# Grouped attention with all output stored in 256 B rows, and the last K block loaded in two halves

## The chip, the cores and the metric

The kernel runs on one core of a Trainium2 chip. The metric is the device time in microseconds (us) of one execution. One core has a matrix engine (PE), a vector engine (DVE), a scalar engine (ACT), a general engine (POOL) and SyncE (SP), which here only issues DMAs; 16 DMA engines move the data.

## The reference, cut to what matters

```python
B, Hq, Hkv, Sq, Sk, D = 16, 32, 8, 16, 2048, 128      # q, k, v in bf16
k = jnp.repeat(k, 4, axis=1);  v = jnp.repeat(v, 4, axis=1)
scores = jnp.einsum("bhqd,bhkd->bhqk", q, k) * D ** -0.5
return jnp.einsum("bhqk,bhkd->bhqd", softmax(scores, axis=-1), v)
```

There are 16 x 8 = 128 pairs of batch and key head. Each pair has 64 query rows, 2048 keys and 2048 values. K and V are 64 MiB each, q and the output 2 MiB each, so the work is mostly a stream of K and V through the chip.

## The kernel before, in words

**Tiling.** The pairs are taken four at a time: 32 quads, numbered n. A quad's K is one DMA of 2 MiB into one of three buffers (`Kn`, `load_k`), its V two DMAs of 1 MiB into one of four buffers (`Vb`, `load_v`). Each quad makes two steps, so there are 64 steps; step 2n works on the first half of the keys, step 2n+1 on the second half.

**A step on the engines.** DVE transposes a half of K (`kt`, L450, two instructions). PE multiplies it with the query matrix (`S`, L372 and L317). DVE scales and negates the scores out of PSUM and finds their minimum (`negated`, L463). ACT takes exponentials (L579). PE transposes the probabilities (`PT`, L392), ACT evicts them (L591), and PE multiplies them with V (`PV`, L421). Five steps lie between the scores of a step and its PV. When a quad's two PVs are done, ACT (in the last steps DVE, `norm`, L535) multiplies the sums by the reciprocal row sums and writes an output buffer `Osb` (L602).

**The query.** For every four quads, POOL lays q out with masks (`lay_q`, L178), PE folds and transposes it (`Q`, L350), and ACT evicts it (`qe`, L567 and L570).

**The output.** There are NO = 8 output buffers. A quad's output is 256 rows of 256 B. For quads below PAIRED = 28 the query rows are arranged so that two neighbouring output rows come out in partitions 32 apart; POOL copies one beside the other (`join`, L198, two copies per quad), and the two stores of the quad (`store_part`, L191) then move 64 pieces of 512 B each. Quads 28 to 31 are stored without joining, in 128 pieces of 256 B per store.

**The order on SP.** SP issues all loads and nearly all stores, in one order written out by a loop over t = 0 to 63 + SLAG (L288). At even t it issues the K of quad t/2, when the buffer's transposes are done; at t = p + 6, or p + 7 from p = 24 on, half p of V, when the PV of the quad four before is done; at even t from SLAG = 20 on, the two stores of quad (t - 20)/2, when its joins are done. The whole last V comes at t = 70 in three pieces of 16, 12 and 4 key blocks (`LASTV`, L265). So the stores of quads 0 to 24 stand ahead of the last V, and those of 25 to 31 behind it. The last store's second half goes out from ACT's own queue.

Of the kernel before, what the change touches and what calls it, by code (L numbers as in the profile page):

```python
# [6 lines left out]
ACT = mybir.ActivationFunctionType  # L7
ALU = mybir.AluOpType
# [4 lines left out]
NK = 3  # L13
# [1 line left out]
NKT = 2  # L15
NS = 3
NPT = 4
NO = 8
NQ = 2
VLAG = (6, 7)  # L20
VFAR = 24
PVLAG = 5
SLAG = 20
PAIRED = 28
QLOAD = (0, 1, 5)
QLEAD = 13
TURNS = 8
# [3 lines left out]
NMBASE = 8  # L31
# [6 lines left out]
def bass_standalone__gqa_softmax__sampling_kernel(  # L38
# [29 lines left out]
    Sneg = [sb(f"Sneg{i}", [128, Sk], F32) for i in range(NS)]  # L68
    P = [sb(f"P{i}", [128, 16, 2, 64], F32) for i in range(2)]
    PT = [sb(f"PT{i}", [128, 8, 128], F32) for i in range(NPT)]  # L70
    Osb = [sb(f"O{i}", [128, 2, 2, 128], BF16) for i in range(NO)]
    nhalf = sb("nhalf", [128, 2, RING], F32)
    nbias = sb("nbias", [128, RING], F32)
    rowsum = sb("rowsum", [128, RING], F32)
# [4 lines left out]
    def col(x, p):  # L79
        return x[:, p % RING:p % RING + 1]  # L80
# [33 lines left out]
    sem_e2 = sem("sem_e2")  # L114
    sem_nm = sem("sem_nm")
    sem_nl = sem("sem_nl")
    sem_pc = sem("sem_pc")

    qf = q.rearrange("b h s d -> (b h s) d")
    of = out.rearrange("b h s d -> (b h s) d")  # L120
# [49 lines left out]
    def pt_ap(h, i):  # L170
        return PT[h % NPT][:, 4 * i:4 * (i + 1), :].rearrange("p t q -> p (t q)")

    def lay_q(eng, c, rs=range(4)):
        if rs[0] == 0:
            eng.wait_ge(sem_q[c % NQ], 16 * (c // NQ + 1))
        src = Qn[c % NQ][:, :, :].rearrange("p j (b x) -> p (j b) x", b=2)
        for r in rs:
            eng.tensor_scalar(  # L178
                Q4[:, :, :, r, :].rearrange("p j b x -> p (j b) x"), src,
                mask[:, r:r + 1], None, op0=ALU.mult,  # L180
            ).then_inc(sem_q4, 1)

    def store_part(eng, n, c):
        rows = of[256 * n + 128 * c:256 * n + 128 * (c + 1), :]
        if n < PAIRED:
            dst = rows.rearrange("(x r l) d -> r x (l d)", x=2, l=2)
            src = Osb[n % NO][64 * c:64 * c + 32, :, :, :].rearrange("p x l d -> p x (l d)")
        else:
            dst = rows.rearrange("(x r) d -> r x d", x=2)
            src = Osb[n % NO][64 * c:64 * (c + 1), :, 0, :]  # L190
        eng.dma_start(dst, src).then_inc(sem_o[n % NO], 16)  # L191

    def join(eng, n):
        eng.wait_ge(sem_nm, NMBASE + 2 * n + 2)
        for c in range(2):
            if 2 * n + c >= 1:
                eng.wait_ge(sem_pc, 2 * n + c)
            eng.tensor_copy(  # L198
                Osb[n % NO][64 * c:64 * c + 32, :, 1, :], Osb[n % NO][64 * c + 32:64 * (c + 1), :, 0, :],
            ).then_inc(sem_pc, 1)  # L200

    with nc.Block() as block:

        @block.gpsimd
        def _(gp):
            gp.iota(iota_m[:, :, :], [[-8, 4], [-32, 4]], base=0, channel_multiplier=1).then_inc(sem_id, 1)
            gp.iota(iota_t[:, :], [[1, 128]], base=0, channel_multiplier=-1).then_inc(sem_id, 1)
            gp.wait_ge(sem_id, 2)
            gp.tensor_scalar(ident4[:, :], iota_t[:, :], 0.0, None, op0=ALU.is_equal).then_inc(sem_id, 1)
            gp.tensor_scalar(lo_m[:, :, :], iota_m[:, :, :], 0.0, None, op0=ALU.is_ge).then_inc(sem_id, 1)  # L210
            gp.tensor_scalar(hi_m[:, :, :], iota_m[:, :, :], 8.0, None, op0=ALU.is_lt).then_inc(sem_id, 1)
            gp.wait_ge(sem_id, 5)
            gp.tensor_tensor(lo_m[:, :, :], lo_m[:, :, :], hi_m[:, :, :], op=ALU.mult).then_inc(sem_id, 1)
            for x in range(2):
                gp.wait_ge(sem_id, 6 + x)
                a = lo_m[:, :, :] if x == 0 else hi_m[:, :, :]
                w = 2 >> x
                dst = hi_m[:, :, 0:2] if x == 0 else mask[:, :].unsqueeze(2)
                gp.tensor_tensor(dst, a[:, :, 0:w], a[:, :, w:2 * w], op=ALU.add).then_inc(sem_id, 1)
            gp.wait_ge(sem_id, 8)  # L220
            id4 = ident4[:, :].rearrange("p (u i r) -> p u i r", u=4, i=4)
            gp.tensor_tensor(half_m, id4[:, :, 0:2, :], id4[:, :, 2:4, :], op=ALU.add).then_inc(sem_id, 1)
            gp.wait_ge(sem_id, 9)
            gp.tensor_tensor(fold[:, :, :], half_m[:, :, 0, :], half_m[:, :, 1, :], op=ALU.add).then_inc(sem_id, 1)
            gp.sem_inc(sem_nm, NMBASE)
            for c in range(1, NQC):
                gp.wait_ge(sem_stq, 2 * c)
                if c >= 3:
                    gp.wait_ge(sem_pc, 8 * c - 16)
                lay_q(gp, c, (0, 1))  # L230
                if c >= 2:
                    gp.wait_ge(sem_q4, 4 * c + 2)
                    join(gp, 4 * c - 8)
                    gp.wait_ge(sem_pc, 8 * c - 14)
                lay_q(gp, c, (2, 3))
                if c >= 2:
                    gp.wait_ge(sem_q4, 4 * c + 4)
                    for n in range(4 * c - 7, 4 * c - 4):
                        join(gp, n)
            for n in range(4 * NQC - 8, PAIRED):  # L240
                join(gp, n)

        @block.sync
        def _(sp):
            def load_k(n):
                s = n % NK
                if n >= NK:
                    sp.wait_ge(sem_kt, 2 * (n - NK) + 2)
                sp.dma_start(Kn[s][:, :], kf[n]).then_inc(sem_k[s], 16)

            def load_v(p):
                n, c = divmod(p, 2)
# [20 lines left out]

            def store(n):
                s = n % NO
                if n < PAIRED:
                    sp.wait_ge(sem_pc, 2 * n + 2)
                elif n < NQD - 2:
                    sp.wait_ge(sem_nm, NMBASE + 2 * n + 2)
                elif n == NQD - 2:  # L280
                    sp.wait_ge(sem_nl, 3)
                else:
                    sp.wait_ge(sem_nm, NMBASE + 2 * (NQD - 2) + 1)
                    sp.wait_ge(sem_nl, 4)
                for c in range(2 if n < NQD - 1 else 1):
                    store_part(sp, n, c)

            for t in range(NT + SLAG):  # L288
                if t == 4:
                    sp.sem_inc(sem_exp, EXPBASE)  # L290
                    sp.sem_inc(sem_e2, TURNS - 1)
                for c in range(NQC):
                    if t == (QLOAD[c] if c < len(QLOAD) else 8 * c - QLEAD):
                        load_q(c)
                if t < NT and t % 2 == 0:
                    load_k(t // 2)
                for p in range(NT):
                    if t == p + VLAG[p >= VFAR]:
                        load_v(p)
                if t >= SLAG and t % 2 == 0:  # L300
                    store((t - SLAG) // 2)
            for s in range(NO):
# [3 lines left out]
        def _(pe):  # L306
# [18 lines left out]
            def emit(op, turn=False):  # L325
# [11 lines left out]
                elif op[0] == "Q":  # L337
# [6 lines left out]
                        wait(sem_ev[b], 8 * c - 4, 8, turn)  # L344
                    dst = ST_ps[:, 512 * b:512 * (b + 1)]
                    src = Q4[:, :, :, :, :].rearrange("p j b i (x e) -> p j b e (i x)", e=2)
                    dst = dst.rearrange("p (u l r j e) -> p j l e u r", u=4, l=2, r=8, j=4)
                    for j in range(8):
                        for e in range(2):
                            ins = pe.matmul(  # L350
                                dst[:, j // 2, j % 2, e], src[:, j, b, e, :], fold[:, :, :], start=True, stop=True)
                    ins.then_inc(sem_stq, 1)
                elif op[0] == "S":
                    _, n = op
# [90 lines left out]
        def _(dve):  # L445
            def kt(n, e, k_at=None):
                Q, x = divmod(n, 2)
                if x == 0 and e == 0:
                    dve.wait_ge(sem_k[Q % NK], 16 * (Q // NK + 1) if k_at is None else k_at)
                ins = dve.transpose(  # L450
                    KT[n % NKT][:, :].rearrange("p (t b g e a) -> p e g t b a", t=8, b=2, g=2, e=2)[:, e],
                    Kn[Q % NK][:, :].bitcast(F32).rearrange(
# [77 lines left out]
            def norm(n, xs, done):  # L530
# [2 lines left out]
                dve.wait_ge(sem_pv, 2 * n + 2)  # L533
                for x in xs:
                    dve.tensor_scalar(  # L535
                        Osb[n % NO][:, x, 0, :], o_ap(n, x), col(rrec, 2 * n + x), None, op0=ALU.mult).then_inc(done, 1)

            def evict(h, halves):
                for i in halves:
# [19 lines left out]
        def _(act):  # L559
            for op in act_prog:  # L560
                if op[0] == "qe":
                    _, c, b = op
                    act.wait_ge(sem_stq, 2 * c + b + 1)
                    dst = QT[:, b, :, :, :].rearrange("p u q e -> p (u q e)")
                    src = ST_ps[:, 512 * b:512 * (b + 1)]
                    if 4 * c < PAIRED:
                        ins = act.activation(dst, src, ACT.Copy)  # L567
                    else:
                        for l in range(2):
                            ins = act.activation(  # L570
                                dst.rearrange("p (u r l e) -> p l u r e", u=4, l=2, e=2)[:, l],
                                src.rearrange("p (u l r e) -> p l u r e", u=4, l=2, e=2)[:, l], ACT.Copy)
                    ins.then_inc(sem_qe, 1)
                elif op[0] == "exp":
                    p, lo, hi = op[1], *(op[2:] or (0, 16))
                    n, x = divmod(p, 2)
# [18 lines left out]
                else:  # L595
                    _, n, x = op
                    if x == 0:
                        act.wait_ge(sem_rec, n + 1)
                        if n >= NO:
                            act.wait_ge(sem_o[n % NO], 32 * (n // NO))  # L600
                        act.wait_ge(sem_pv, 2 * n + 2)
                    act.activation(Osb[n % NO][:, x, 0, :], o_ap(n, x), ACT.Copy,  # L602
                                   scale=col(rrec, 2 * n + x)).then_inc(sem_nm, 1)
            act.wait_ge(sem_nm, NMBASE + 2 * (NQD - 2) + 1)
            act.wait_ge(sem_nl, 4)
# [29 lines left out]
```

## Time and profile before

| | |
|---|---|
| median of 3 runs | 337.86 us (337.86 to 337.90) |
| the profiled execution, its own time | 337.53 us |
| its span, first to last instruction | 335.7 us |
| busy: PE, DVE, ACT, POOL | 280.0, 308.0, 220.6, 104.1 us |
| DMA packets and bytes | 21151 packets, 138.62 MB, mean 413 GB/s |
| join copies, POOL L198 | 56, mean 393 ns |

All times inside the span count from its first instruction. The device time is 1.8 us longer than the span. A busy share is an average over the span; what sets the end is read from the chain of waits, which goes back from the last instruction, at each step to what released it. A packet is what one DMA engine moves at a time; the trace lists for each its queue, start, duration and size, and for each DMA when its semaphore was raised (it landed).

### The profile page before, as it was taken

The page shows a single profiled execution, that of the slowest core. Times are in us where ns is not written, and L with a number is a line of the kernel's source. Part 1 is how long each engine was busy: PE and PEld are TensorE (multiplying, and loading weights), DVE is VectorE, ACT ScalarE, POOL GpSimd, SP SyncE. Part 2 cuts the span into 40 slices and gives each one's busy share as a digit, 9 for nine tenths or more (in the row PEclk, how much of TensorE's full clock was granted, in tenths as well). Part 3 has the DMA queues.
Part 4 walks back from the last instruction along what each step waited for, and adds up shares of the span by engine and source line. Part 5 has one row for each costly group of instructions (what it writes and reads, how often), then busy time and mean ns, then how long its engine had stood idle before and what let it go on. Part 6 is the DMA issues. An engine that isn't in the chain of part 4 may idle for free.

```text
span 335.7 us, 14448 instructions
## 1 busy us (share of the span) xinstructions
PE 280.0 (83%) x6959; PEld 158.3 (47%) x5893; DVE 308.0 (92%) x465; ACT 220.6 (66%) x331; POOL 104.1 (31%) x98
## 2 busy tenths in 40 slices
PE   7877678888988899888988898878877979777895
PEld 2013344445545555455644554444543545444575
DVE  1999998998999999999999999899999999999872
ACT  2044666766787677766777677756767757567671
POOL 3840037300680029400680029400592000000000
PEclk9999999999999999999999999999999999999999
DMA  7999999999999999999999999999999999999995
GB/s 293 443 418 428 424 416 412 423 424 426 415 420 418 424 431 422 423 428 417 414 428 427 424 424 414 422 427 429 422 419 420 423 427 428 420 427 412 422 411 177
DMA packets 21151, 138.62 MB, mean 413 GB/s; under 512 B 3728, under 2 KB 7568, under 8 KB 9104
## 3 DMA queue, kind: packets, MB, share of 16 engines
q1 hardware_dynamic: 20992, 138.39, 99.3%
q8 instruction: 9, 0.15, 0.2%
q10 hardware_dynamic: 144, 0.03, 0.1%
q14 instruction: 6, 0.05, 0.0%
HBM read 136.31 MB, written 2.10 MB: 412 GB/s over the span
## 4 chain that ended last, share of the span: by engine, by line
DVE 49%; DMA 28%; PE 17%; issue 3%; ACT 2%; DVEq 0%
DMA Kn<-in_k_dram 27%; DVE Sneg L463 25%; DVE KT L450 22%; PE S_ps L372 5%; PE S_ps L317 4%; PE O_ps L421 3%; PE ST_ps L392 2%; PE ST_ps L350 2%; ACT P L579 1%; PE O_ps L317 1%; DMA Qn<-in_q_dram 1%; PE S_ps L421 1%; DVE Q L178 1%; ACT PT L591 0%; DVE nbias L472 0%
## 5 line engine op out<-in xcount | busy, mean ns | idle before, releaser
L450 DVE STREAM_TRANSPOSE KT<-Kn 128x1024 f32<-128x1024 f32 x128 | 151.0, 1218 | 10.3 <-DMA Kn<-in_k_dram 10.3
L463 DVE TENSOR_SCALAR_CACHE_REDUCE Sneg<-S_ps 128x1024 f32<-128x1024 f32 x128 | 149.9, 1205 | 4.9 <-PE S_ps L317 4.4
L579 ACT ACTIVATE P<-Sneg,nbias 128x2048 bf16<-128x2048 f32 (+1 forms) x66 | 129.0, 1955 | 15.4 <-DVE nbias L472 15.2
L372 PE MATMUL S_ps<-KT,QT 32*64 32x512 bf16 x1024 | 106.5, 387 | 35.4 <-DVE Sneg L463 34.4
L591 ACT ACTIVATE PT<-ST_ps 128x512 f32<-128x512 f32 x123 | 66.7, 597 | 60.2 <-PE ST_ps L392 60.2
L317 PE MATMUL S_ps<-KT,QT 32*64 32x512 bf16 x1024 | 106.0, 381 | 0.0
L178 POOL TENSOR_SCALAR Q<-Qn,mask 128x1024 bf16<-128x1024 bf16 x28 | 79.2, 2842 | 48.3 <-PE ST_ps L350 42.2
L372 PEld LDWEIGHTS S_ps<-KT,QT 32*64 32x64 bf16 x1024 | 34.8, 103 | 104.3 <-issue 91.3
L421 PEld LDWEIGHTS O_ps<-Vb,PT 64*64 64x64 bf16 x3968 | 58.0, 107 | 49.1 <-issue 48.7
L421 PE MATMUL O_ps<-Vb,PT 64*64 64x128 bf16 x3968 | 67.9, 218 | 14.4 <-DMA Vb<-in_v_dram 12.4
L198 POOL COPY O<-O 32x256 bf16<-32x256 bf16 x56 | 22.0, 393 | 163.9 <-ACT O L602 145.7
L392 PE MATMUL ST_ps<-ident,P 128*128 128x128 f32 x512 | 69.9, 280 | 0.2 <-ACT P L579 0.2
L392 PEld LDWEIGHTS ST_ps<-ident,P 128*128 128x128 f32 x512 | 54.8, 141 | 8.4 <-issue 2.6
L602 ACT ACTIVATE O<-O_ps,rrec 128x128 bf16<-128x128 f32 x56 | 17.5, 363 | 22.1 <-PE O_ps L421 22.1
L567 ACT ACTIVATE QT<-ST_ps 128x512 bf16<-128x512 f32 x14 | 7.7, 595 | 9.1 <-PE ST_ps L350 9.0
L579 ACT ACTIVATION_READ_ACCUMULATOR P<-Sneg,nbias 128x1 f32 x66 | 13.3, 201 | 0.0
L350 PEld LDWEIGHTS ST_ps<-fold,Q 128*128 128x128 bf16 x256 | 8.5, 101 | 7.9 <-issue 7.9
L317 PE MATMUL O_ps<-ident 128*128 128x512 bf16 x42 | 11.2, 415 | 0.0
L463 DVE DVE_READ_ACCUMULATOR Sneg<-S_ps 128x1 f32 x128 | 10.5, 82 | 0.0
L350 PE MATMUL ST_ps<-fold,Q 128*128 128x32 bf16 x256 | 9.4, 198 | 0.3 <-DVE Q L178 0.3
L472 DVE TENSOR_TENSOR nbias<-nhalf 128x2 f32<-128x2 f32 x32 | 5.3, 167 | 1.1
L459 DVE RECIPROCAL rrec<-rowsum 128x2 f32<-128x2 f32 x31 | 4.9, 159 | 0.0
(27 smaller groups left out, 19.9 us busy)
## 6 DMA issues: line engine op xcount, KB each, us to landing
Kn<-in_k_dram SPq DMA_DIRECT2D x32, 2048.0 KB, 18.2
Vb<-in_v_dram SPq DMA_DIRECT2D x63, 1024.0 KB, 21.4
Qn<-in_q_dram SPq DMA_DIRECT2D x8, 256.0 KB, 16.1
out_dram<-O SPq DMA_DIRECT2D x63, 32.0 KB, 19.8
Vb<-in_v_dram SPq DMA_DIRECT2D x1, 768.0 KB, 14.4
Vb<-in_v_dram SPq DMA_DIRECT2D x1, 256.0 KB, 14.6
out_dram<-O ACTq DMA_DIRECT2D x1, 32.0 KB, 2.0
```

What stands on the lines that cost most here:

```text
L178: eng.tensor_scalar(Q4[:, :, :, r, :].rearrange("p j b x -> p (j b) x"), src, mask[:, r:r + 1], None, op0=ALU.mult,).then_inc(sem_q4, 1)
L198: eng.tensor_copy(Osb[n % NO][64 * c:64 * c + 32, :, 1, :], Osb[n % NO][64 * c + 32:64 * (c + 1), :, 0, :],).then_inc(sem_pc, 1)
L317: return pe.add_instruction(mybir.InstMatmult(name=nc.get_next_instruction_name(), engine=mybir.EngineType.PE, ins=[pe.lower_ap(rhs), pe.l ...
L350: ins = pe.matmul(dst[:, j // 2, j % 2, e], src[:, j, b, e, :], fold[:, :, :], start=True, stop=True)
L372: ins = pe.matmul(s_ap, w, x, start=(acc == 0), stop=(acc == 3))
L392: ins = pe.transpose(dst[:, 128 * z:128 * (z + 1)], src[:, t, :], ident4[:, :])
L421: ins = pe.matmul(o_ap(n, x)[64 * c:64 * (c + 1), :], w[rows, c], Vb[n % NV][rows, c, key, :], start=(key == 0), stop=(key == 31),)
L450: ins = dve.transpose(KT[n % NKT][:, :].rearrange("p (t b g e a) -> p e g t b a", t=8, b=2, g=2, e=2)[:, e], Kn[Q % NK][:, :].bitcast(F32) ...
L463: ins = dve.tensor_scalar(Sneg[p % NS][:, 1024 * x:1024 * (x + 1)].rearrange("p (t a m) -> p t a m", t=8, m=4), S_ps[:, 1024 * y:1024 * (y ...
L579: ins = act.activation(P[n % 2][:, lo:hi, x, :].bitcast(BF16), Sneg[p % NS][:, 128 * lo:128 * hi].rearrange("p (t k) -> p t k", k=128), AC ...
L591: act.activation(pt_ap(h, i), stage_ap(h, i), ACT.Copy).then_inc(sem_ev[i], 1)
L602: act.activation(Osb[n % NO][:, x, 0, :], o_ap(n, x), ACT.Copy, scale=col(rrec, 2 * n + x)).then_inc(sem_nm, 1)
```

## The change

- The output is stored for all quads in rows of 256 B, 128 pieces per store. `join` goes from POOL, and the arrangement of the query rows that it needed goes from PE's `Q` and ACT's `qe`: PE now writes its folded query in runs of 32 columns, and ACT reorders while it evicts.
- There are ten output buffers in place of eight, and the stores come 24 steps behind the loads in place of 20. The stores of quads 0 to 22 then stand ahead of the last V and those of 23 to 31 behind it.
- The last K (quad 31) is loaded in two DMAs of 1 MiB, one for each step, each with two pieces of 4 KiB per partition. Between them goes the V half that followed the whole K before (half 55). The second half has its own semaphore.
- A start value of a semaphore is added by SP in place of POOL.

```diff
-NO = 8
+NO = 10
-SLAG = 20
-PAIRED = 28
+SLAG = 24
-    Osb = [sb(f"O{i}", [128, 2, 2, 128], BF16) for i in range(NO)]
+    Osb = [sb(f"O{i}", [128, 2, 128], BF16) for i in range(NO)]
     def store_part(eng, n, c):
-        rows = of[256 * n + 128 * c:256 * n + 128 * (c + 1), :]
-        if n < PAIRED:
-            dst = rows.rearrange("(x r l) d -> r x (l d)", x=2, l=2)
-            src = Osb[n % NO][64 * c:64 * c + 32, :, :, :].rearrange("p x l d -> p x (l d)")
-        else:
-            dst = rows.rearrange("(x r) d -> r x d", x=2)
-            src = Osb[n % NO][64 * c:64 * (c + 1), :, 0, :]
-        eng.dma_start(dst, src).then_inc(sem_o[n % NO], 16)
+        dst = of[256 * n + 128 * c:256 * n + 128 * (c + 1), :].rearrange("(x r) d -> r x d", x=2)
+        eng.dma_start(dst, Osb[n % NO][64 * c:64 * (c + 1), :, :]).then_inc(sem_o[n % NO], 16)
# SP, load_k and the loop over t
-                sp.dma_start(Kn[s][:, :], kf[n]).then_inc(sem_k[s], 16)
+                if n < NQD - 1:
+                    sp.dma_start(Kn[s][:, :], kf[n]).then_inc(sem_k[s], 16)
+                else:
+                    load_k_half(0)
+            def load_k_half(x):
+                n = NQD - 1
+                halves = lambda t: t.rearrange("a (g x y) -> a x g y", g=2, x=2)[:, x]
+                sp.dma_start(halves(Kn[n % NK][:, :]), halves(kf[n])).then_inc(sem_kl if x else sem_k[n % NK], 16)
                 for p in range(NT):
                     if t == p + VLAG[p >= VFAR]:
                         load_v(p)
+                if t == NT - 2:
+                    load_k_half(1)
# SP, store
-                if n < PAIRED:
-                    sp.wait_ge(sem_pc, 2 * n + 2)
-                elif n < NQD - 2:
+                if n < NQD - 2:
                     sp.wait_ge(sem_nm, NMBASE + 2 * n + 2)
# DVE, kt
+                if n == NT - 1 and e == 0:
+                    dve.wait_ge(sem_kl, 16)
```

More of the change, by code (lines that the diff above doesn't have):

```diff
@@ L116, in bass_standalone__gqa_softmax__sampling_kernel @@
     sem_nl = sem("sem_nl")
-    sem_pc = sem("sem_pc")
+    sem_kl = sem("sem_kl")
     qf = q.rearrange("b h s d -> (b h s) d")
@@ L171, in pt_ap, with lay_q @@
         return PT[h % NPT][:, 4 * i:4 * (i + 1), :].rearrange("p t q -> p (t q)")
-    def lay_q(eng, c, rs=range(4)):
-        if rs[0] == 0:
-            eng.wait_ge(sem_q[c % NQ], 16 * (c // NQ + 1))
+    def lay_q(eng, c):
+        eng.wait_ge(sem_q[c % NQ], 16 * (c // NQ + 1))
         src = Qn[c % NQ][:, :, :].rearrange("p j (b x) -> p (j b) x", b=2)
-        for r in rs:
+        for r in range(4):
             eng.tensor_scalar(
@@ L183, in store_part @@
     def store_part(eng, n, c):
-        rows = of[256 * n + 128 * c:256 * n + 128 * (c + 1), :]
-        if n < PAIRED:
-            dst = rows.rearrange("(x r l) d -> r x (l d)", x=2, l=2)
-            src = Osb[n % NO][64 * c:64 * c + 32, :, :, :].rearrange("p x l d -> p x (l d)")
-        else:
-            dst = rows.rearrange("(x r) d -> r x d", x=2)
-            src = Osb[n % NO][64 * c:64 * (c + 1), :, 0, :]
[L191 to L200, printed above, removed]
+        dst = of[256 * n + 128 * c:256 * n + 128 * (c + 1), :].rearrange("(x r) d -> r x d", x=2)
+        eng.dma_start(dst, Osb[n % NO][64 * c:64 * (c + 1), :, :]).then_inc(sem_o[n % NO], 16)
     with nc.Block() as block:
@@ L224, in _ @@
             gp.tensor_tensor(fold[:, :, :], half_m[:, :, 0, :], half_m[:, :, 1, :], op=ALU.add).then_inc(sem_id, 1)
-            gp.sem_inc(sem_nm, NMBASE)
             for c in range(1, NQC):
                 gp.wait_ge(sem_stq, 2 * c)
[L228 to L241, printed above, removed]
+                lay_q(gp, c)
         @block.sync
@@ L289, in _ @@
                 if t == 4:
+                    sp.sem_inc(sem_nm, NMBASE)
                     sp.sem_inc(sem_exp, EXPBASE)
@@ L346, in emit @@
                     src = Q4[:, :, :, :, :].rearrange("p j b i (x e) -> p j b e (i x)", e=2)
-                    dst = dst.rearrange("p (u l r j e) -> p j l e u r", u=4, l=2, r=8, j=4)
+                    mv = fold[:, :, :].rearrange("p u r -> p (u r)")
                     for j in range(8):
                         for e in range(2):
-                            ins = pe.matmul(
-                                dst[:, j // 2, j % 2, e], src[:, j, b, e, :], fold[:, :, :], start=True, stop=True)
+                            z = 2 * j + e
+                            ins = pe.matmul(dst[:, 32 * z:32 * (z + 1)], src[:, j, b, e, :], mv, start=True, stop=True)
                     ins.then_inc(sem_stq, 1)
@@ L535, in norm @@
                     dve.tensor_scalar(
-                        Osb[n % NO][:, x, 0, :], o_ap(n, x), col(rrec, 2 * n + x), None, op0=ALU.mult).then_inc(done, 1)
+                        Osb[n % NO][:, x, :], o_ap(n, x), col(rrec, 2 * n + x), None, op0=ALU.mult).then_inc(done, 1)
             def evict(h, halves):
@@ L563, in _ @@
                     act.wait_ge(sem_stq, 2 * c + b + 1)
[L564 to L573, printed above, removed]
+                    act.activation(
+                        QT[:, b, :, :, :].rearrange("p u (r j) e -> p (u r) (j e)", j=8),
+                        ST_ps[:, 512 * b:512 * (b + 1)].rearrange("p (z a) -> p a z", z=16), ACT.Copy,
+                    ).then_inc(sem_qe, 1)
                 elif op[0] == "exp":
@@ L601, in _ @@
                         act.wait_ge(sem_pv, 2 * n + 2)
-                    act.activation(Osb[n % NO][:, x, 0, :], o_ap(n, x), ACT.Copy,
+                    act.activation(Osb[n % NO][:, x, :], o_ap(n, x), ACT.Copy,
                                    scale=col(rrec, 2 * n + x)).then_inc(sem_nm, 1)
```

## The prediction

> **What bounds the kernel now.** First the page's slices and queues.
>
> ```profile
> DMA  7999999999999999999999999999999999999995
> ...
> q1 hardware_dynamic: 20992, 138.39, 99.3%
> ```
>
> From the second slice to the last but one the DMA engines are never idle, and SP's queue holds nearly all their time. What a DMA costs there moves everything behind it. Second, the chain of waits, its last 51 us (start, length, what).
>
> ```profile
> 284.80 23.30 DMA Kn<-in_k_dram
> 308.10 0.02 issue
> 308.12 2.37 DVE KT L450 x2
> 310.49 2.28 DVE Sneg L463 x4
> ...
> 312.87 2.36 DVE KT L450 x2
> 315.24 2.28 DVE Sneg L463 x4
> ...
> 328.07 2.06 PE O_ps L421 x128
> 330.13 0.32 issue
> 330.45 2.01 PE S_ps L421 x128
> ...
> 332.58 0.35 DVE O L535
> ```
>
> The last K lands at 308.10. DVE and PE work through it, the last PV (S_ps L421) ends at 332.46, the last output is scaled, and at 333.05 SP issues the last store, which lands at 335.26. The trace's landings show a second bound close by: the three pieces of the last V land at 328.82, 330.78 and 331.53, and PE needs them at 330.45, 331.45 and 332.2, only 0.7 us later for the latter two. Third, SP's own order of time and the group of stores (minimum/median/maximum ns).
>
> ```profile
> 300.07 4.94 SPq L191 DMA_DIRECT2D out_dram<-O  x2
> 305.90 1.64 SPq L258 DMA_DIRECT2D Vb<-in_v_dram  x2
> 307.58 3.18 SPq L191 DMA_DIRECT2D out_dram<-O  x2
> 315.96 1.90 SPq L265 DMA_DIRECT2D Vb<-in_v_dram  x3
> 317.91 15.73 SPq L191 DMA_DIRECT2D out_dram<-O  x13
> ```
> ```profile
> L191 SPq DMA_DIRECT2D out_dram<-O x63: 425/433/4315, 83.1 to 333.0; - x63
> ```
>
> A store's issue takes 0.43 us, but some last up to 4.3 us without waiting for a semaphore: the first behind the last V 3.18 us (317.91 to 321.10). I counted the packets that SP had issued and no engine had started: in such issues those of all earlier DMAs come to 70 to 83 per engine when the issue ends. I read that as a queue that takes no more. One thing more: the stores of 256 B at 327.62, 328.26, 330.92 and 333.05 take 0.59 to 0.63 us to issue, with little queued for the last two.
>
> **Part by part. The stores.** Packets of 512 B take 27.2 ns among the loads. The first 105 packets of 256 B, in the full queue at 329 us, take 18.0 ns each. The landings of K lie 9.88 us apart without stores and 10.06 with a quad's two. Packet durations give these times if each packet overlaps the next by 3.6 ns: 256 x 309.4 + 128 x 612.4 + 48 x 5.4 ns over 16 engines is 9.87 us, and a quad's stores 128 x 23.6 + 32 x 5.4 over 16 add 0.20. In rows of 256 B a quad costs 256 x 14.4 + 32 x 5.4 over 16 = 0.24 us. Bounds: 11.8 ns (half a 512 B packet) gives 0.20, as before; 23.6 ns (as long as a 512 B packet) gives 0.39; the mean of all 256 B packets of this queue, 20.9 less 3.6, gives 0.29. I take 14.4, the row in the full queue.
>
> Two quads of stores fewer stand ahead of the end's loads. Ahead of the last V: 23 x 0.24 - 25 x 0.20 = +0.55 us. The last K in pieces of 4 KiB: 512 x (160.5 - 3.6) against 128 x 612.4 ns, over 16, +0.12. So the last V is 0.7 us later. The K of quad 30 (stores of 18 quads ahead, not 20) is 0.35 later, the last K 0.4.
>
> **The last K.** Before, DVE is done with quad 30's steps at 307.52 and idles 0.60 us until 308.12. Quad 30's work now ends at 307.9. The first half, 256 x 156.9 ns over 16 = 2.5 us after the V that ends at 303.2 + 0.4, lands at 306.1, so DVE goes straight on at 307.9, 0.25 earlier than before. The second half lands after one V (2.5) and its own 2.5 at 311.1; it is wanted at 312.6, so the new wait costs nothing. Behind that wait on DVE stand the last two negations and PE's S; were it late by x, the chain would be too. The last PV could start at 330.2, but the last V's pieces now come at 331.5 and 332.2, and the final 16 products end at about 332.5. The gain is eaten: compute ends where it did.
>
> **POOL, PE, ACT.** The 56 joins (22.0 us) go. POOL is not in the chain, and the stores wait 6.5 us in all for it while the DMA engines are full: nothing. ACT's query eviction (595 ns, in the reordered form of the last four quads 2 x 390) becomes one that the trace doesn't show: between 0.6 us and, at twice the reordered form, 1.6 us. I take 0.8. It comes twice in eight steps, and ACT is idle a third of the span, so even 1.6 is hidden; the first lies under the first K's landing (8.79). PE's L350 keeps its count. The two further output buffers keep the old distance: store n-10 at t = 2n+4, as n-8 was. SP's addition to a semaphore comes before its third K, at under 3 us; PV needs it far later.
>
> **SP's queue at the end.** Here I find the cost. Behind the last V stood 13 store issues on SP; now there are 17, all in 9 packets per engine (8 and a semaphore) where most had 5, and each takes 0.60 + 0.045 us, not 0.43 + 0.045. The last V itself holds 51 packets per engine. With 83 let in, SP places the fourth store behind it only when the DMAs before the V are nearly through (about 327 us), the sixth when 13 packets of the first piece are (328.5 to 329), the eighth when 31 are (330.7 to 331.2). Nine are left, and the last starts eight issues later: 330.75 + 8 x 0.645 = 335.9, against 333.05. That is +2.85. The same count makes the tail of before 0.7 us late (store 28's second half ends at 327.0, the trace says 326.35) and the first stalled issue 0.5 early; I take off 0.35 and forecast **+2.5**. Bounds: 100 let in instead of 83 gives +1.7, 76 gives +3.4; issues of 0.50 us give +2.0; 256 B packets by their mean give +3.9.
>
> The Trainium skill, DMA: Bandwidth & Descriptors, "Issuing engines are not separate DMA queues", says that starting DMAs on several engines saves only the sequencer's time, usually small beside the DMA itself; by that SP's issuing would add nothing. The rows here disagree for stores this small: 0.60 us of issue against 0.12 us of the engines' time.
>
> **The rivals.**
> 1. *256 B packets cost as 512 B ones.* Each then counts 23.6 ns: 23 x 0.39 - 25 x 0.20 + 0.12 = +4.1 for the last V, and SP's queue behind it comes to +6.2: 344.1; halfway +4: 341.9. For it: only 105 packets in a full queue show 18 ns, and later ones 18 to 25. Against: all 105 do. The skill's same page, "Specifications", has 512 B as the least transfer at line rate, below which the engine reads, modifies and writes; that speaks for this rival, and the 18.0 ns row against.
> 2. *SP keeps up.* If the queue took 128 packets, the last store would not wait for SP (-0.2 by the same count), and the last V sets the end at 0 to +0.4: 338.1. For it: in places 95 to 100 counted packets lie there. Against: issues of 3 to 4 us.
> 3. *Faster: the earlier K half decides.* If 256 B packets cost the line no more than half a 512 B one (11.8 ns) and SP keeps up, then the last K comes earlier by two quads of stores (0.4) and DVE's idle 0.6 goes, so PE is 1.0 ahead; the last V, 0.27 earlier, lets it use its slack of 0.65 besides: 0.9 in all, 337.0. It decides from the point where the last V is less than 0.65 late (just under 14.4 ns a packet) and SP can issue the last store as soon as it is scaled. Against: the 18.0 ns row and SP's stalls both have to be wrong.
>
> **The numbers.** Against the profiled execution (span 335.7, time 337.53) the forecast is 340.0; that execution is 0.33 below the median, so the median becomes 337.86 + 2.5 = 340.4. The forecast has 0.60 (339.2 to 341.8), rival 1 0.15 (341.9 to 344.1), rival 2 0.15, rival 3 0.10. The range leaves out rival 3 and the dearer half of rival 1: 337.8 to 342.6. With 0.2% (0.7 us) as the least that can be told from no change: faster 0.10, same 0.15, slower 0.75.
>
> **What would show it.** Right: after the last V a row of store issues on SP with no gap, 0.6 us each, the last at 335 to 336, and the last PV ending at 332 to 333, long before. K's landings 10.10 to 10.11 us apart where stores go. DVE without idle time before the last K's first transpose. Wrong: the last store issued right after the last scaling (rival 2 or 3), or K's landings 10.2 us apart or more (rival 1).

## The result, and the profile after

| | before | after |
|---|---|---|
| median | 337.69 us (12 runs, 337.43 to 337.90) | 338.74 us (12 runs, 338.21 to 339.35) |
| profiled execution, its own time | 337.53 us | 338.54 us |
| its span | 335.7 us | 336.7 us |
| SP's issue of the last store | 333.05 | 334.28 |
| that store lands | 335.26 | 336.21 |

The ratio is 1.0031 (95% interval 1.0022 to 1.0040): the changed kernel is slower by 1.05 us, 0.3%. The forecast was +2.5, in the same direction and with the same cause, but more than twice too large.

The page of after, slices and queue, in the form shown for before:

```profile
DMA  7999999999999999999999999999999999999996
...
q1 hardware_dynamic: 24976, 138.39, 99.6%
```

SP's queue moves the same bytes in 24976 packets in place of 20992, and the engines are as full as before. The chain of waits of after, its last part (start, length, what):

```profile
314.05 1.05 PE O_ps L399 x61
315.10 0.02 issue
315.12 0.39 SPq L242
315.51 0.04 issue
315.55 15.53 DMA Vb<-in_v_dram
331.08 0.14 issue
331.22 1.11 PE S_ps L399 x64
...
332.45 0.35 DVE O L515
```

Before, the chain's last DMA was the last K. Now it is the second piece of the last V: PE waits for it until 331.22, and the last output is scaled at 332.8, against 332.9 before. So the computation ends no later. But this chain goes back from the last instruction of a computing engine, and the span ends 3.9 us behind that, where in before it was 2.8 us. What lies there is in SP's order of time of after (start, length, the same kind merged):

```profile
312.04 1.58 SPq L183 DMA_DIRECT2D out_dram<-O  x2
315.12 3.50 SPq L242 DMA_DIRECT2D Vb<-in_v_dram  x3
318.66 16.22 SPq L183 DMA_DIRECT2D out_dram<-O  x17
```

From 318.66 to 334.88 SP does nothing but issue stores, 17 of them with no gap. In before 13 took 15.73 us from 317.91 on, with two longer waits for outputs that were not yet scaled. The stores' line in after (minimum/median/maximum ns) shows the price:

```profile
L183 SPq DMA_DIRECT2D out_dram<-O x63: 596/717/7073, 101.1 to 334.3; - x63
```

No store issues in under 596 ns, where 425 was the least before. And the last K, in DVE's order of time of after:

```profile
307.22 0.16 DVE L439 RECIPROCAL rrec<-rowsum 128x2 f32<-128x2 f32 x1
307.29 2.35 DVE L430 STREAM_TRANSPOSE KT<-Kn 128x1024 f32<-128x1024 f32 x2
```

The transposes of the last K start at 307.29 without idle time (before: 308.12, after 0.60 us of waiting). DVE is 0.83 us earlier, and PE gives all of it back waiting for the last V.

### The profile page after: what moved, and what is told of

Same layout as the page of the kernel before. It is cut to its first block, busy times and chain, and to the rows that moved or that the text cites. A ratio compares the mean times of both kernels' runs of the same rounds, so it can differ in the third digit from the quotient of the medians.

```text
span 336.7 us, 14364 instructions
## 1 busy us (share of the span) xinstructions
PE 279.2 (83%) x6959; PEld 156.8 (47%) x5893; DVE 307.6 (91%) x465; ACT 220.2 (65%) x329; POOL 82.0 (24%) x42
## 3 DMA queue, kind: packets, MB, share of 16 engines
q1 hardware_dynamic: 24976, 138.39, 99.6%
## 4 chain that ended last, share of the span: by engine, by line
DVE 49%; DMA 35%; PE 9%; issue 4%; SPq 2%; DVEq 0%
DVE Sneg L443 25%; DVE KT L430 23%; DMA Vb<-in_v_dram 19%; DMA Kn<-in_k_dram 16%; PE S_ps L350 3%; PE S_ps L295 2%; PE O_ps L399 2%; PE ST_ps L370 1%; SPq L235 1%; SPq L219 1%; PE S_ps L399 0%; DVE rrec L439 0%; DVE nbias L452 0%; PE ST_ps L329 0%; DVEq L485 0%
## 5 line engine op out<-in xcount | busy, mean ns | idle before, releaser
L544 ACT ACTIVATE QT<-ST_ps 128x512 bf16<-128x512 f32 x16 | 8.7, 595 | 8.7 <-PE ST_ps L329 8.7
L329 PEld LDWEIGHTS ST_ps<-fold,Q 128*128 128x128 bf16 x256 | 7.0, 97 | 7.9 <-issue 7.9
L329 PE MATMUL ST_ps<-fold,Q 128*128 128x32 bf16 x256 | 7.8, 178 | 0.3 <-DVE Q L176 0.3
L176 DVE TENSOR_SCALAR Q<-Qn,mask 128x1024 bf16<-128x1024 bf16 x4 | 1.7, 481 | 3.5 <-DMA Qn<-in_q_dram 3.5
```

Of the source, the lines that this page charges most:

```text
L176: eng.tensor_scalar(Q4[:, :, :, r, :].rearrange("p j b x -> p (j b) x"), src, mask[:, r:r + 1], None, op0=ALU.mult,).then_inc(sem_q4, 1)
L329: ins = pe.matmul(dst[:, 32 * z:32 * (z + 1)], src[:, j, b, e, :], mv, start=True, stop=True)
L544: act.activation(QT[:, b, :, :, :].rearrange("p u (r j) e -> p (u r) (j e)", j=8), ST_ps[:, 512 * b:512 * (b + 1)].rearrange("p (z a) -> p ...
```

## The experiments

Theory Q: SP's row of store issues behind the last V sets the end. Theory V: rows of 256 B load the DMA queue and so delay the last V. Each kernel was measured beside before, whose median was then 337.56 to 337.64 us; the ratios are to that before.

**Eight forms of the three parts.** Rows, steps and halves were put together in all ways (the diffs are those of the change, part by part; nine buffers with joined rows and 24 steps, since ten don't fit beside them).

| rows | steps | last K | kernel | median us | ratio to before (95%) |
|---|---|---|---|---|---|
| 512 B | 20 | whole | before | 337.56 to 337.69 | |
| 256 B | 20 | whole | `rows_only` | 337.85 | 1.0005 (0.9996 to 1.0014) |
| 512 B | 24 | whole | `b_slag24` | 337.56 | 0.9999 (0.9990 to 1.0008) |
| 512 B | 20 | halves | `b_halves` | 337.38 | 0.9992 (0.9983 to 1.0001) |
| 512 B | 24 | halves | `b_halves_slag24` | 337.46 | 0.9997 (0.9988 to 1.0006) |
| 256 B | 20 | halves | `a_slag20` | 337.57 | 0.9997 (0.9989 to 1.0006) |
| 256 B | 24 | whole | `a_wholek` | 338.46 | 1.0027 (1.0018 to 1.0037) |
| 256 B | 24 | halves | after | 338.74 | 1.0031 (1.0022 to 1.0040) |

Only two of them are slower, those with 256 B rows and 24 steps together. Neither part costs anything that can be measured alone, and the halves have no share in the loss that can be told from noise. What was expected of each:

`rows_only` (PAIRED and `join` gone, SLAG 20, NO 8):

> The stores of 256 B without joining alone: whole last K, 20 steps, eight buffers. Theory Q: 13 issues behind the last V, of 0.65 us in place of 0.48 to 0.65; SP just keeps up, within 0.4 us of before, 337.5 to 338.1 us. Theory V: all of the change's loss comes from the rows, 0.04 us or more for each of 25 quads ahead of the last V, 338.6 us or more.

`a_slag20`:

```diff
-SLAG = 24
+SLAG = 20
```

> After, with the stores 20 steps behind as in before (ten buffers kept): 13 issues behind the last V. Theory Q: SP is free before the last output is scaled; the last V with two more quads of stores ahead is 0.3 to 0.4 us later, and the end comes 0.8 to 1.2 us earlier than in after, 337.5 to 337.9 us. Theory V: 0.3 to 0.4 us later than after, 339.1 us.

`b_slag24` (before with SLAG 24, NO 9):

> Before, with the stores 24 steps behind and nine buffers (more don't fit beside the joined rows), joined as before: 17 issues behind the last V, ten of them of 512 B rows. Theory Q in its form of a price per issue: these cost 0.48 us and 5 packets each, SP is done before the last output is scaled, and compute sets the end as in before: 337.4 to 337.7 us. Rival (the number of stores behind the last V is enough, whatever their rows): as after, 338.5 us or more.

`b_halves` (before with the diff's `load_k_half` and the wait in `kt`):

> Before, with the last K in two halves and nothing else. Theory Q, with the last V as the next bound: DVE and PE are 0.6 to 0.8 us ahead, the last V is 0.2 us later by the 4 KiB pieces, PE waits for it, and the end moves by -0.4 to 0.0 us against before: 337.2 to 337.6 us. Rival (the halves bring their whole 0.6 us, or cost): 337.0 us, or 337.9 us and more.

`b_halves_slag24`:

> Before, with the last K in halves and the stores 24 steps behind, rows joined: the change without its rows of 256 B. Theory Q: SP keeps up, the last V is 0.1 to 0.2 us earlier than in before and sets the end: 337.1 to 337.4 us. Rival (halves and late stores are what costs): 338.5 us or more.

`a_wholek` (after without `load_k_half` and its wait):

> After, with the last K loaded whole: rows of 256 B and 24 steps together, without the halves. Theory Q: SP's 17 issues of 0.60 us and more set the end as in after, 338.3 to 338.8 us. Rival (the halves are needed for the loss, by their packets in SP's queue): 337.9 us or less.

All came out as theory Q had it, `b_halves_slag24` 0.06 us above its window. Theory V falls: it wanted rows alone to cost 1 us, and 20 steps to be worse than 24. That SP keeps up with joined rows and 24 steps is seen in `b_halves_slag24`: the eighth store issue behind the last V ends at 325.57, in after at 328.53, and SP is done with all but the last store at 331.14, 1.3 us before that one can go. `b_halves` also shows why the halves bring so little. Its chain of waits, the end:

```profile
315.79 15.29 DMA Vb<-in_v_dram
331.07 0.14 issue
331.21 1.11 PE S_ps L432 x61
...
332.45 0.35 DVE O L548
```

It is the chain of after, nearly to the hundredth: the wait for the last K is gone, the wait for the last V stands 0.1 to 0.2 us ahead of where K's chain ended. SP has time there, and the 0.2 us reach the median, if at all: the interval just touches 1.

**More stores behind the last V.** `a_slag28` is after with two numbers changed:

```diff
-NO = 10
+NO = 12
-SLAG = 24
+SLAG = 28
```

> After, with the stores 28 steps behind and 12 output buffers: two more quads of stores behind the last V, 21 issues on SP in place of 17. Theory Q: four more issues of 0.65 us, 2.6 us later than after, 340.8 to 341.5 us. Theory V: two quads of stores fewer ahead of the last V, 0.3 to 0.4 us earlier, 338.4 us.

Measured: 341.81 us, ratio 1.0121 (1.0106 to 1.0135), 3.07 us over after and 0.3 over theory Q's window. SP's order of time of this kernel:

```profile
314.87 3.72 SPq L242 DMA_DIRECT2D Vb<-in_v_dram  x3
318.64 19.61 SPq L183 DMA_DIRECT2D out_dram<-O  x21
```

The last V landed 0.28 us earlier than in after and the last output was scaled 0.26 us earlier (332.19 in place of 332.45), yet the last store was issued at 337.65, 3.37 us later: four more issues of 0.65 us, and one that lasted 1.5 us in place of 0.6. A last V that comes earlier is worth nothing while SP is late.

**The same stores from two queues.** `a_acttail` is after with the second half of quads 27 to 30 issued by ACT, which has nothing else to do from 327.5 us on:

```diff
-                for c in range(2 if n < NQD - 1 else 1):
+                for c in range(2 if n < ACTQ else 1):          # ACTQ = 27
...
-                 ("pe", L + 3, 0), ("norm", NQD - 1, 0)]
+                 ("pe", L + 3, 0), *(("out", n) for n in range(ACTQ, NQD - 1)), ("norm", NQD - 1, 0)]
```

> After, with the second halves of the stores of quads 27 to 30 issued by ACT in place of SP, so 13 in place of 17 issues stand behind the last V on SP. Theory Q (SP's row of store issues sets the end): the last store goes out as soon as it is scaled, 1.0 to 1.4 us earlier than in after, 337.3 to 337.8 us, and SP waits before it. Theory V (the end is later because rows of 256 B delay the last V): SP's issues don't matter, as after, 338.7 us.

Measured: 337.53 us, ratio 1.0003 (0.9993 to 1.0013), 1.21 us under after. SP's and ACT's order of time:

```profile
318.68 14.89 SPq L184 DMA_DIRECT2D out_dram<-O  x13
```
```profile
326.86 3.94 ACTq L184 DMA_DIRECT2D out_dram<-O  x4
332.51 0.37 ACT L584 ACTIVATE O<-S_ps,rrec 128x128 bf16<-128x128 f32 x1 [5.06 <-PE S_ps L400]
332.97 0.64 ACTq L184 DMA_DIRECT2D out_dram<-O  x1
```

The loss is gone: the last store is issued at 332.97, as soon as it is scaled. The four stores also go through ACT's DMA queue in place of SP's (720 packets there, 144 in after). That gave SP no earlier start: its eighth issue behind the last V ends at 328.62, in after at 328.53. What is gone are four of the nine issues that followed. Together with `a_slag28` this settles theory Q.

**Looking for a faster one.** Three versions tried to bring the last V forward. `a_slag26_act` is `a_acttail` with these numbers (from `a_acttail` to it):

```diff
-NO = 10
+NO = 11
-SLAG = 24
+SLAG = 26
-ACTQ = 27
+ACTQ = 26
```

> After, with the stores 26 steps behind, eleven buffers, and the second halves of quads 26 to 30 issued by ACT. Theory Q: SP has 14 issues behind the last V and just keeps up; the last V is 0.2 us earlier than with 24 steps: 337.2 to 337.5 us. Rival (SP's row is late again, or ACT's issues hold up its evictions): 338.0 us or more.

`a_slag26_act`: 337.66 us, 1.0005 (0.9996 to 1.0014), over its window. The second piece of the last V landed 0.54 us earlier than in `a_acttail` (330.56, not 331.10) and the last store was issued at 332.45 in place of 332.97, but it landed 2.93 us later, not 2.20. Its issue took 1.11 us in place of 0.60, and 13 packets per engine stood ahead of it in SP's queue, in `a_acttail` 2. The work was moved, not saved.

`b_halves_slag24_act` is `b_halves_slag24` with ACT's part of `a_acttail`, from quad 28 on (ACTQ = 28).

> Before, with the last K in halves, 24 steps, rows joined, nine buffers, and the second halves of quads 28 to 30 issued by ACT. Theory Q: SP was no longer the bound without ACT's help, so the end stays with the last V: 337.2 to 337.5 us. Rival (SP's issues still cost here): 336.9 us.

`b_halves_slag24_act`: 337.42 us, 0.9998 (0.9989 to 1.0007). As expected, ACT's help is worth nothing where SP keeps up.

`b_halves_slag28_act` differs from it in one number:

```diff
-SLAG = 24
+SLAG = 28
```

> The same with the stores 28 steps behind, nine buffers: two more quads behind the last V. If the last V is the bound and SP keeps up: 0.3 to 0.4 us earlier than with 24 steps, 336.9 to 337.1 us. If SP's row is late again (18 issues, 14 of them of 0.48 us) or ACT waits for a buffer: 337.5 to 338.5 us.

`b_halves_slag28_act`: 339.95 us, 1.0071 (1.0058 to 1.0085), worse than either window. Its waits (engine, line, waited for, us in total, times, longest):

```profile
ACT O L623 <- DMA out_dram<-O: 39.4, 17, 3.2
```

With 28 steps and nine buffers ACT waits 17 times for a store to empty the buffer it is to write, and the computation falls behind: the last output is scaled at 335.04, though the second piece of the last V lands at 330.65, in before at 330.78. No version beat before by more than the measurement is uncertain.

## Why the prediction was right in kind and wrong in size

**What bounds the kernel**: right. The DMA engines are full up to the last slice in both, and the slack of 0.7 us between the last K's chain and the last V decided what the halves were worth.

**Rows of 256 B in the queue**: sized at the wrong end of its bounds. K's landings where stores go mostly lie 10.07 to 10.08 us apart, against 10.06 before and 9.88 to 9.90 without stores. A quad's stores cost 0.19 us, against 0.18: nearly the lower bound (11.8 ns, as before), not 14.4. The packets do last 18.0 ns each, as the 105 did, 18 by the median of all 8064; by my way of adding up they overlap by some 7 ns, not 3.6. Rival 1 asked for 10.2 us or more and is out. The Trainium skill's row that spoke for it (DMA: Bandwidth & Descriptors, "Specifications": 512 B as the least transfer at line rate) is not borne out here as a price: 0.19 us against 0.18.

**The last K's halves**: right in effect. DVE goes straight on and the second half is never late. The 4 KiB pieces cost 0.19 us (5.11 for both halves, 4.92 for the whole), not 0.12. The last V came 0.3 us later in the profiled execution, forecast 0.7. That 0.3 need not come from the change: single intervals, which differ from one execution to the next, are off by as much. One between two landings of K in before is 10.34, mostly they are 10.07; one V in after takes 2.88, mostly 2.56.

**POOL, PE, ACT**: right. POOL's joins (22 us) go and nothing moves. The query's eviction costs 595 ns, as in the contiguous form.

**SP's queue at the end**: the right mechanism, and the step that failed is in it: the moment at which SP places the eighth store behind the last V, "the eighth when 31 are (330.7 to 331.2)". In after the eighth issue ends at 328.53, 2.2 us before the 330.75 that went into the sum. The fourth and the sixth are early too (324.96 and 327.03, forecast about 327 and 328.5 to 329). Some 0.4 us of the 2.2 is the last V, which I had put 0.7 us late and which came 0.3 us late. The rest is a count read off the wrong times.

The limit itself held: when the sixth and the eighth issue end, the packets of earlier DMAs still waiting come to 81 and 85 per engine, against my 83. But I had measured this as a mean over the 16 engines and then used it with the landing times, which are those of the slowest engine. The engines are far apart: the semaphore of the last V's first piece is raised by one engine at 326.54 and by the last at 329.12. The mean engine has begun its 13th packet of these pieces at 326.73 and its 31st at 328.78. From there my own count gives 328.78 + 0.05 + 8 x 0.645 = 334.0 for the start of the last store's issue, against 335.9 in the prediction. Measured is 334.28, 1.23 us later than before; that store landed 1.93 us after its issue began, before 2.21, and the remaining 0.95 us is what the span shows (+1.0). The check against before, where the count came out 0.7 late at store 28, was the hint, and I took off only half of it.

The Trainium skill's rule weighed there (DMA: Bandwidth & Descriptors, "Issuing engines are not separate DMA queues") says two things. That only the sequencer's time is saved fits. That this time is usually small beside the DMA does not hold for this tail: an issue takes 0.60 us where the engines' time is 0.1 us, and four issues moved to ACT are worth 1.2 us.

**The rivals**: rival 2 (SP keeps up) is what happens in all versions with 20 steps or 512 B rows. Of rival 3 the first condition was met (11 ns a packet). Its gain of 0.9 us was not seen where SP keeps up as well: with 256 B rows `a_slag20` and `a_acttail` are 0.07 and 0.11 us under the before that ran beside them, and with 512 B rows `b_halves` and `b_halves_slag24` are 0.23 and 0.15 us under it, none of them clear of noise. Rival 3 let the last V come 0.27 us earlier. Its second piece landed at 331.33 in `a_slag20` and 331.10 in `a_acttail`, against 330.78 in before.

What stays open: how the price of 256 B rows in the tail divides between the longer issue (596 ns against 425) and the nine packets per engine in place of five. The versions change both at once. Part of it the trace of after does show: behind the eighth issue the packets waiting fall from 85 per engine to under 10, and the issues last 0.60 to 0.68 us all the same, one 0.95. There the length of the issue is what counts; in the eight before them both may.

## What to carry to other kernels

A chain of waits that ends with a computing engine does not show an issuing queue that is still at work: look at how long the span goes on behind it, and at the issuing engine's own order of time. Two edits that are free alone can cost together when both lengthen the same row of instructions, so count what a change puts behind the last load, in issues and in packets, not in bytes. When a count is a mean over 16 engines, don't read its times off landings, which belong to the slowest of them.

## What the runs showed of the hardware that was not expected

- The least issue time of a store of 32 KB on SP is 425 to 426 ns in 64 pieces of 512 B (one issue of 342 ns in `b_halves_slag28_act` apart) and 595 to 597 ns in 128 pieces of 256 B, in every kernel of the study; the engines' own time for it is some 100 ns (an estimate: half of the 0.19 us that a quad's two stores add between K's landings).
- Halving the piece of a store in a full queue costs nearly nothing in the engines' time: 0.19 us per quad in place of 0.18.
- In after a store's issue whose output had been scaled 54 us before lasted 7.1 us, while the earlier DMAs' packets waiting fell from 95 to 77 per engine. One without any semaphore to wait for lasted 5.2 us.
- The 16 engines finish one DMA up to 2.6 us apart in the steady stream of after (up to 2.5 us in before).
